# The first scaling of raw weight words in the attention stage, made by GpSimd

## The chip, the cores and the metric

The kernel runs on one core of one Trainium2 chip. A core has TensorE (PE, matmuls; PEld is its weight load), VectorE (DVE), ScalarE (ACT), GpSimd (POOL) and SyncE (SP, which issues DMAs). The metric is the device time of one execution in microseconds; the kernel before takes 1007.44 us (median of 3 runs, 1006.85 to 1007.59).

## The reference, cut to what matters

Attention with a cumulative bias, then two feed-forward layers, the first with a product of two projections, the second with a squared ReLU:

```python
scores = scale * q @ k.T                      # 4 batches, 8 heads, S = 576, D = 64
scores = where(causal, -1e9, scores + minimum(cum_j - cum_i, 0))   # cum: cumsum(relu(s))
x = softmax(scores) @ v                       # -> 2304 tokens x 512
x = ((x @ w_a) * (x @ w_b)) @ w_out           # 512 -> 1536 -> 512
r = maximum(x @ w_in2, 0)                     # 512 -> 2048
out = (r * r) @ w_out2                        # -> 512
```

The weights come in as double precision numbers, that is as pairs of 32-bit words, and are made on the chip into a high and a low part of single precision.

## The kernel before, in words

**Arithmetic.** Every large matmul is made of three: high by high, high by low, low by high. So each operand is held twice. The low parts come from a subtraction of the rounded high part.

**Decoding a weight block.** A block of 128 x 512 weights is decoded by `words` (L1002) and `decode` (L1031), in this chain: SP loads 512 KB of raw words; the high words, read as floats, are scaled by 2^-112 in place (the "first scaling", L1015: by DVE or ACT, whichever the planner finds free sooner); DVE shifts and masks the high words into a new tile, then merges the sign; the low words are scaled by 2^-29 (ACT or DVE); POOL or DVE adds them in; ACT casts the sum to the high part `wh`; POOL or DVE subtracts for the low part (`wl`, `wlo`). The first layer has 36 such blocks, `split_w(f)` for f = 0 to 11, each with its three matrices; the raw words lie in tiles named `words`, `roomxh` and `roomxl`. The loads of the first six blocks (f below 2) are `held`. The second layer's blocks go through `quarters` (L1061), which calls `words` too: those of w_in2 in a stream called "late" (tiles `w2ir`), those of w_out2 later (tiles `w2or`).

**Stages by time.** 0 to 50 us: attention of the first batch. 50 to about 395: the first feed-forward layer on the first chunks of tokens, whose weight blocks are decoded as they are needed, woven with the attention of the second to fourth batch and with the "late" decoding of the second layer's w_in2. To 640: the rest of the first layer. 640 to 1010: the second layer, whose `first` (L1526) loads two prepared blocks of w_in2 (`w_3_0`, `w_3_1` from scratch `w2q`) and makes the products `pa`, `pb`, `pc`, and whose `second` multiplies by w_out2 (tiles `ws_*` from `w2s`) into `po_*`. `quads` (L1306) loads the second layer's inputs (`yr`) and splits them.

**Names.** In the instruction orders below the leading digit of a name (batch, chunk) is left out and a running number follows: `ab_9_0` is the w_a product of weight block f = 9, `g_8` the gated result of block 8, `py` the first layer's output product, `st` and `se` scores, `pt` and `tt` transposed exponentials, `av` and `ae` weighted values, `tav` the same for the first batch's last rows, `rs` the transpose of the row sums, `yd` the first layer's output on its way to the second.

**What sets the order.** Nothing of the order is written by hand. `Plan` (L73) records every operation with the engines that may make it and a cost for each, and `order` (L148) simulates the engines with those costs and sorts all operations by their planned start; L267 then issues them. The costs for n elements a row are 150 + each x n ns on DVE, 190 + 0.833 n on ACT, 110 + 2.3 n on POOL, and 3 ns for each KB of a load. A cost is thus no time, but it decides which engine makes an operation and when each is issued. Where the plan lets PE idle for over `GAP` (400 ns) before the first product into a fresh bank, `order` notes idle/`BURN` (230 ns) matmuls on a constant tile, and L262 issues them there ("warm" matmuls):

```python
gap = t - max(free[e], min(op.bank.tag.free))
if gap > self.GAP:
    op.idle = max(op.idle, int(gap / self.BURN))
...
for _ in range(op.idle if warm else 0):
    w = warm.get()
    eng.matmul(op.bank.get(), w[:, : w.shape[0]], w, start=True, stop=True)
```

Of the kernel before, what the change touches and what calls it, by code (L numbers as in the profile page):

```python
# [7 lines left out]
F32 = mybir.dt.float32  # L8
# [5 lines left out]
ALU = mybir.AluOpType  # L14
# [255 lines left out]
def attention_moe_moe(tc, q, k, v, s, w_a, w_b, w_out, w_in2, w_out2, out):  # L270
# [18 lines left out]
    CW = 384  # L289
# [18 lines left out]
    pl = Plan(nc)  # L308
# [27 lines left out]
    def scratch(shape, dtype, name):  # L336
        return pl.fixed(lambda: pools["dram"].tile(shape, dtype, name=name))
# [17 lines left out]
    def on_dve(method, n, *args, two=False, each=1.04, **kw):  # L355
        return "DVE", 150 + each * n, two, method, args, kw

    def on_act(method, n, *args, psum=False, **kw):
        return "ACT", (155 if psum else 190) + 0.833 * n, False, method, args, kw

    def on_gps(method, n, *args, **kw):
        return "POOL", 110 + 2.3 * n, True, method, args, kw

    def dve(*args, reads=(), **kw):
        pl.call(on_dve(*args, **kw), reads=reads)
# [7 lines left out]
    def dma(out, in_, kb, takes=(), lag=0.0):  # L373
        pl.call(("SP", max(kb * 3.0, 170.0), False, "dma_start", (out, in_), {}), takes=takes, lag=lag)
# [5 lines left out]
    def copy(n, out, in_, psum=False, by="AD"):  # L380
        ways = []
        if "A" in by:
            ways.append(on_act("copy", n, out, in_, psum=psum))
        if "D" in by:
            ways.append(on_dve("tensor_copy", n, out, in_, two=not psum, each=1.04 if psum else 0.52))
        pl.call(*ways)

    def subtract(n, out, a, b, by="PD"):
        kw = {"out": out, "in0": a, "in1": b, "op": ALU.subtract}
        ways = []  # L390
        if "P" in by:
            ways.append(on_gps("tensor_tensor", n, **kw))
        if "D" in by:
            ways.append(on_dve("tensor_tensor", n, two=True, **kw))
        pl.call(*ways)
# [590 lines left out]
    def quad(nm):  # L986
        return gated("lop", [P, 2 * CW], F32R, "yq", 14, nm)
# [14 lines left out]
    def words(w, by_col, f, raw, t, takes=(), held=False):  # L1002

        f0 = 2 * f * P
        n = ND * P
        if by_col:
            src = w[:, f0 : f0 + 2 * P].rearrange("(d p) c -> p d c", p=P)
        else:
            src = w[f * P : f * P + P, :].rearrange("p (d c) -> p d c", d=ND)
        dma(raw.rearrange("p (d c) -> p d c", d=ND), src, 540 if pl.stream == "late" else 680, takes, HOLD if held else 0.0)  # L1010
        pairs = raw.rearrange("p (n w) -> p n w", w=2)
        low, high = pairs[:, :, 0], pairs[:, :, 1]

        hf = high.bitcast(F32)
        pl.call(  # L1015
            on_dve("tensor_scalar", n, hf, hf, 2.0**-112, None, op0=ALU.mult, two=True, each=0.52),
            on_act("mul", n, hf, hf, 2.0**-112),
        )
        dve(
            "tensor_scalar", n, t, high, 3, 0x7FFFFFF8, op0=ALU.logical_shift_left, op1=ALU.bitwise_and, two=True,  # L1020
            each=0.52,
        )
        dve("scalar_tensor_tensor", n, t, high, -0x80000000, t, op0=ALU.bitwise_and, op1=ALU.bitwise_or, two=True)
        pl.call(
            on_act("activation", n, low, low.bitcast(U32), AF.Copy, scale=2.0**-29),
            on_dve("tensor_scalar", n, low, low.bitcast(U32), 2.0**-29, None, op0=ALU.mult, two=True, each=0.52),
        )
        kw = {"out": t, "in0": t, "in1": low, "op": ALU.add}
        pl.call(on_gps("tensor_tensor", n, **kw), on_dve("tensor_tensor", n, two=True, **kw))
# [12 lines left out]
    w2q = [[scratch([P, 7 * QW], F32, f"w2q{j}_{z}") for z in range(2)] for j in range(PAIRS)]  # L1042

    def temp(dtype, nm):
        return gated("lop", [P, 2 * DM], dtype, "tmp", 4, nm)
# [260 lines left out]
    def quads(nm, source):  # L1306

        n = 2 * CW

        def pull(k, h):  # L1310
            x = temp(F32, f"yr{nm}_{k}{h}")[:, :n]
            for d in range(2):
                for at_, m, src in source(2 * k + d, h):
                    dma(x[:, d * CW + at_ : d * CW + at_ + m], src, m * 0.5)
            return x

        b11, b21, b22, b12 = (pull(k, h) for k, h in ((0, 0), (1, 0), (1, 1), (0, 1)))
        lo, hi = {}, {}

        def split(x, v):  # L1320
            lo[x], hi[x] = quad(f"{x}l{nm}"), quad(f"{x}h{nm}")
            copy(n, hi[x], v)
            subtract(n, lo[x], v, hi[x].bitcast(F32))

        split("b11", b11)
        split("b21", b21)
        split("b22", b22)
        combine(n, b22, b22, b12)
        combine(n, b12, b12, b11)
        combine(n, b11, b11, b22, ALU.add)  # L1330
        combine(n, b21, b21, b11)
        for x, v in (("t2", b11), ("t1", b12), ("t3", b22), ("t4", b21)):
            split(x, v)
        return {x: [t[x].rearrange("p (d c) -> p d c", d=2) for t in (hi, lo)] for x in hi}
# [191 lines left out]
    def first(t0, j, left, held):  # L1526

        nm = f"{t0}_{j}"
        pair = j % 2
        yq = y_quads[t0]  # L1530
        w = [block(f"w{nm}_{z}") for z in range(2)]
        for z in range(2):
            dma(w[z].rearrange("p q c -> p (q c)").bitcast(F32), w2q[j][z], 896)

        def times(ps, q, start=True):
            i = SEVEN.index(q)
            product(ps, [[x[:, i, d * P : d * P + P] for d in range(2)] for x in w], yq[q], start)

        def bank_(k):
            if t0 == 0 and j == 1:  # L1540
                return gated("po", [P, 512], F32, "po", 5, f"p{k}{nm}")[:, :CW]
            return mm_bank(f"p{k}{nm}")[:, :CW]

        v1, v3 = (x[:, :CW] for x in halves(f"v{nm}a", F32))
        v2, v4 = (x[:, :CW] for x in halves(f"v{nm}b", F32))

        def squared(v, ps, s):
            if s is None:
                urgent(act, "activation", CW, v, ps, AF.Relu, psum=True)
            else:  # L1550
                urgent(dve, "tensor_tensor", CW, out=v, in0=ps, in1=s, op=ALU.add)
                pl.call(
                    on_act("activation", CW, v, v, AF.Relu),
                    on_dve("tensor_scalar_max", CW, v, v, 0.0, two=True, each=0.52),
                )
            kw = {"out": v, "in0": v, "in1": v, "op": ALU.mult}
            pl.call(on_act("activation", CW, v, v, AF.Square), on_dve("tensor_tensor", CW, two=True, **kw))
            return v

        def split(q, v):  # L1560
            if q in ROOM:
                if pair == 0:
                    held[q] = flat(ROOM[q], 1, f"g{nm}{q}")
                hi, lo = (held[q][:, 2 * pair + z, :CW].part((pair, z)) for z in range(2))
            else:
                hi, lo = (flat("wh", 3 * NF1, f"g{nm}{q}{z}")[:, :CW] for z in range(2))
            left[q, pair] = hi, lo
            copy(CW, hi, v, by="A")
            subtract(CW, lo, v, hi.bitcast(F32))

        def keep(tag, bufs, width, k, ps):
            t = sb([P, width], F32, tag, bufs, f"{k}{nm}")[:, :CW]
            urgent(act, "copy", CW, t, ps, psum=True)
            return t

        a = bank_("a")
        times(a, "b11")
        s1 = keep("a", 2, 512, 1, a)
        b = bank_("b")
        times(b, "b21")  # L1580
        b11 = squared(v1, b, s1)
        times(a, "t2", False)
        s2 = keep("lo1", 1, DM, 2, a)
        b = bank_("c")
        times(b, "t1")
        times(a, "t3", False)
        s3 = keep("a", 2, 512, 3, a)
        b22 = squared(v3, b, s3)
        times(a, "t4", False)
        b21 = squared(v2, a, None)  # L1590
        times(b, "b22", False)
        b12 = squared(v4, b, s2)
        split("b11", b11)
        split("b22", b22)
        split("b21", b21)
        combine(CW, b22, b22, b12)
        combine(CW, b12, b12, b11)
        combine(CW, b11, b11, b22, ALU.add)
        combine(CW, b21, b21, b11)
        for q, v in (("t3", b22), ("t1", b12), ("t2", b11), ("t4", b21)):  # L1600
            split(q, v)
# [113 lines left out]
    for t0 in range(0, NT, 2 * CW):  # L1715
        for j in range(PAIRS):
            if j % 2 == 0:
                left, held = {}, {}
# [56 lines left out]
```

## Time and profile before

| | |
|---|---|
| median of 3 runs | 1007.44 us (1006.85 to 1007.59) |
| the profiled execution | 1012.5 us, its span 1010.7 us, mean TensorE clock 0.996 |
| busy in the span | PE 98%, PEld 85%, DVE 73%, ACT 58%, POOL 35% |
| DMA | 242.94 MB, mean 240 GB/s |

The profiled execution is 5.1 us longer than the median of the runs, and 1.8 us of it lie outside the span. Terms worked out from the trace are added to the profiled execution, and the sum is carried to the median. PE is busy almost all the time, so what counts is the few stretches in which it idles or has a lower clock, and whatever is put on PE or taken from it.

### The profile page before, as it was taken

Reading aid. Unit: us, or ns where it says so; the run is one execution under the profiler, and the core shown is the slowest. Engines: PE = TensorE matmul, PEld = TensorE weight load, DVE = VectorE, ACT = ScalarE, POOL = GpSimd, SP = SyncE. Lnnn points to the kernel's source line nnn. Section 1 sums busy time; section 2 is a strip of 40 time slices with the busy share of each in tenths; the row PEclk is TensorE's granted clock in tenths of the full one; section 3 lists DMA queues with packets and bytes.
Section 4 is the critical chain, followed back from the end, with each engine's and each line's share of the span. In section 5 each row is a group of like instructions: output and inputs, shape, how many; then the busy total and the mean of one; then the engine's idle time right before and its main releaser. Section 6 shows DMA issues by size and latency. Waiting matters only on the chain.

```text
span 1010.7 us, 16505 instructions
## 1 busy us (share of the span) xinstructions
PE 990.0 (98%) x5565; PEld 854.8 (85%) x5568; DVE 733.0 (73%) x1499; ACT 584.1 (58%) x1289; POOL 350.4 (35%) x317
## 2 busy tenths in 40 slices
PE   9999999999999999999999999999989999999998
PEld 5567777777777787888889999999989999999998
DVE  5887787867678677386888886657877755876566
ACT  6776776656565564242444443666656766657552
POOL 2543444443344533020233332314544221531122
PEclk9999999999999999999999999999999999999999
DMA  7677787587788778767577557587979976688664
GB/s 218 188 224 243 237 264 237 167 260 240 225 236 252 209 218 265 234 180 264 170 255 229 184 174 275 177 303 253 359 276 328 314 271 229 235 286 301 230 238 167
DMA packets 136972, 242.94 MB, mean 240 GB/s; under 512 B 16204, under 2 KB 87992, under 8 KB 136888
## 3 DMA queue, kind: packets, MB, share of 16 engines
q1 hardware_dynamic: 133688, 235.99, 70.8%
q10 hardware_dynamic: 3200, 5.90, 2.3%
q8 instruction: 44, 0.72, 0.3%
q14 instruction: 40, 0.33, 0.1%
HBM read 183.78 MB, written 52.11 MB: 233 GB/s over the span
## 4 chain that ended last, share of the span: by engine, by line
PE 89%; DMA 5%; DVE 3%; ACT 1%; issue 1%; SPq 1%; POOL 0%; ACTq 0%; DVEq 0%; POOLq 0%
PE ab L267 18%; PE py L267 10%; PE pa L267 9%; PE po_0t L267 6%; PE st L267 5%; PE pc L267 5%; PE wa L267 5%; PE pw L267 4%; PE pt L267 3%; PE av L267 3%; PE wc L267 2%; PE pb L267 2%; PE po_0b L267 2%; PE po_1b L267 2%; PE po_3b L267 2%; PE po_2b L267 1%
## 5 line engine op out<-in xcount | busy, mean ns | idle before, releaser
L267 PE MATMUL py<-g,wh 128*128 128x512 f32 x288 | 92.2, 401 | 0.0
L267 PE MATMUL ab<-xh,wh 128*128 128x512 f32 x192 | 77.6, 404 | 0.0
L267 PE MATMUL ab<-xh,lo 128*128 128x512 f32 x192 | 75.1, 391 | 0.0
L267 PE MATMUL ab<-xl,wh 128*128 128x512 f32 x192 | 74.8, 390 | 0.0
L267 PE MATMUL ab<-x,wh 128*128 128x512 f32 x192 | 64.1, 414 | 0.6 <-POOL x L267 0.6
L267 PEld LDWEIGHTS py<-g,wh 128*128 128x128 f32 x288 | 53.5, 191 | 11.2 <-issue 0.7
L267 DVE CUSTOM_DVE_ANT_0 st<-st,mask 128x512 f32<-128x512 f32 (+2 forms) x96 | 46.7, 502 | 21.3 <-PE st L267 16.2
L267 PE MATMUL py<-g,loo 128*128 128x512 f32 x144 | 56.7, 394 | 0.0
L267 PE MATMUL st<-fk,fq 65*128 65x384 f32 (+3 forms) x128 | 42.5, 443 | 0.9 <-ACT a L267 0.7
L267 ACT COPY a<-ab 128x512 f32<-128x512 f32 x36 | 21.2, 588 | 38.0 <-PE ab L267 37.9
L267 POOL TENSOR_TENSOR w2ip<-w2it,w2ip 128x512 fp32r<-128x512 f32 (+1 forms) x20 | 22.8, 1147 | 58.5 <-ACT w2ip L267 38.4
L267 PEld LDWEIGHTS ab<-xh,lo 128*128 128x128 f32 x192 | 36.0, 188 | 7.8
L267 PE MATMUL av<-ph,val 128*64 128x512 f32 (+3 forms) x256 | 41.5, 445 | 0.0
L267 DVE COPY ph<-pt 128x512 f32<-128x512 f32 (+1 forms) x53 | 31.1, 588 | 14.1 <-PE pt L267 11.9
L267 PEld LDWEIGHTS ab<-xl,wh 128*128 128x128 f32 x192 | 36.2, 189 | 5.9
L267 PEld LDWEIGHTS ab<-xh,wh 128*128 128x128 f32 x192 | 36.2, 188 | 5.9
L267 ACT COPY ph<-pt 128x512 f32<-128x512 f32 (+1 forms) x43 | 22.3, 527 | 31.6 <-PE pt L267 23.5
L267 PEld LDWEIGHTS ab<-x,wh 128*128 128x128 f32 x192 | 33.4, 189 | 7.7 <-issue 1.8
L267 PEld LDWEIGHTS av<-ph,val 128*64 128x64 f32 x256 | 15.5, 136 | 26.4 <-issue 23.7
L267 PE MATMUL ab<-x,wl 128*128 128x512 f32 x96 | 37.8, 394 | 0.0
L267 DVE TENSOR_TENSOR ab<-ab,a 128x512 f32<-128x512 f32 x36 | 25.1, 697 | 16.8 <-PE ab L267 13.9
L267 POOL TENSOR_TENSOR wl<-roomxl,wh 128x512 fp32r<-128x512 f32 x19 | 25.8, 1359 | 30.3 <-ACT wh L267 23.1
(743 smaller groups left out, 3300.0 us busy)
## 6 DMA issues: line engine op xcount, KB each, us to landing
w<-w2q SPq DMA_DIRECT2D x48, 896.0 KB
lo<-wlab SPq DMA_DIRECT2D x36, 512.0 KB
w2q<-w2ip SPq DMA_DIRECT2D x48, 256.0 KB
w2s<-w2op SPq DMA_DIRECT2D x48, 256.0 KB
loo<-wlo SPq DMA_DIRECT2D x24, 384.0 KB
w2ir<-in_moe_w_in SPq DMA_DIRECT2D x16, 512.0 KB
w2or<-in_moe_w_out SPq DMA_DIRECT2D x16, 512.0 KB
ws_0t<-w2s SPq DMA_DIRECT2D x12, 512.0 KB
```

The source lines that it names most:

```text
L267: getattr(eng, method)(*map(real, args), **{k: real(a) for k, a in kw.items()})
```

## The change

Three edits. The first scaling in `words` is given to POOL alone, unless the stream is "late" or the load is held: 34 scalings (30 blocks f = 2 to 11, and four of w_out2). In `quads` the planner's cost of the input loads goes from 0.5 to 0.3 of their width, and in `first` that of the w_in2 loads from 896 to 760; both change no transfer, only the planner's idea of it.

```diff
--- before.py
+++ after.py
@@ -1013,8 +1013,10 @@
 
         hf = high.bitcast(F32)
         pl.call(
+            *((on_gps("tensor_scalar", n, hf, hf, 2.0**-112, None, op0=ALU.mult),) if pl.stream != "late" and not held else (
             on_dve("tensor_scalar", n, hf, hf, 2.0**-112, None, op0=ALU.mult, two=True, each=0.52),
             on_act("mul", n, hf, hf, 2.0**-112),
+            )),
         )
         dve(
             "tensor_scalar", n, t, high, 3, 0x7FFFFFF8, op0=ALU.logical_shift_left, op1=ALU.bitwise_and, two=True,
@@ -1311,7 +1313,7 @@
             x = temp(F32, f"yr{nm}_{k}{h}")[:, :n]
             for d in range(2):
                 for at_, m, src in source(2 * k + d, h):
-                    dma(x[:, d * CW + at_ : d * CW + at_ + m], src, m * 0.5)
+                    dma(x[:, d * CW + at_ : d * CW + at_ + m], src, m * 0.3)
             return x
 
         b11, b21, b22, b12 = (pull(k, h) for k, h in ((0, 0), (1, 0), (1, 1), (0, 1)))
@@ -1530,7 +1532,7 @@
         yq = y_quads[t0]
         w = [block(f"w{nm}_{z}") for z in range(2)]
         for z in range(2):
-            dma(w[z].rearrange("p q c -> p (q c)").bitcast(F32), w2q[j][z], 896)
+            dma(w[z].rearrange("p q c -> p (q c)").bitcast(F32), w2q[j][z], 760)
 
         def times(ps, q, start=True):
             i = SEVEN.index(q)
```

The first place is on PE in the attention of the second batch, about 166 us, where the products of weight block 9 begin. Before:

```order
L267 MATMUL ae_2_2008<-tph_2_0_1992,val_2_1599 64x64 x8
L267 MATMUL ae_2_2008<-tph_2_1_1996,val_2_1599 64x64 x2
L267 MATMUL rs_2_2021<-ident,one_2_1800 9x128
L267 MATMUL ab_8_1_1998<-x_549,wh_1_1789 128x512 x2
L267 MATMUL ab_8_1_1998<-x_549,wl_1754 128x512
L267 MATMUL ab_9_0_2034<-x_406,wh_0_1924 128x512 x2
L267 MATMUL ab_9_0_2034<-x_406,wl_1943 128x512
L267 MATMUL ab_8_1_1998<-x_696,wh_1_1789 128x512 x2
```

After, with the first two of sixteen warm pairs shown and the rest left out:

```order
L267 MATMUL ab_8_1_1959<-x_859,wh_1_1877 128x512 x2
L267 MATMUL ab_8_1_1959<-x_859,wl_1859 128x512
L267 MATMUL ae_2_2001<-tph_2_0_1990,val_2_1598 64x64 x8
L267 MATMUL ae_2_2001<-tph_2_1_1992,val_2_1598 64x64 x2
L267 MATMUL rs_2_2016<-ident,one_2_1805 9x128
L262 LDWEIGHTS warm
L262 MATMUL ab_9_0_2046<-warm 128x512
...
L267 MATMUL ab_9_0_2046<-x_406,wh_0_2036 128x512 x2
L267 MATMUL ab_9_0_2046<-x_406,wl_2041 128x512
```

The products of block 8 now stand ahead of the transpose `rs_2`, and sixteen warm matmuls between it and block 9. ACT's order around the cast of block 9's high part (`wh_0`), before:

```order
L267 COPY ph_2_1_0_1910<-pt_2_1_0_1889 128x512
L267 COPY a_7_1918<-ab_7_0_1771 128x512
L267 CAST wh_0_1924<-roomxl 128x512
L267 ACTIVATE te_2_1937,sum_209<-se_2_0_1878,neg_204 128x288
L267 ACTIVATE te_2_1937,sum_209<-se_2_1_1884,neg_204 128x288
L267 CAST wh_1_1956<-roomxl 128x512
```

And after:

```order
L267 COPY u_2_2019<-av_2_1939 128x512
L267 COPY rows_2_2024<-rs_2_2016 9x128
L267 CAST g_8_2026<-ab_8_1_1959 128x512
L267 CAST wh_0_2036<-roomxl 128x512
L267 CAST wh_1_2039<-roomxl 128x512
```

The cast stood ahead of the exponentials `te` of the second batch; now it stands behind the copy of the transposed row sums and the cast of `g_8`. The second place is on PE where the third batch's attention begins, about 210 us. Before:

```order
L267 MATMUL st_0_1_1_2502<-t2k_0_1_2403,t2q_0_1_2398 128x128
L267 MATMUL pt_0_0_0_2514<-ident,a_0_0_2481 128x128 x2
L267 MATMUL pt_0_0_0_2514<-ident,b_0_0_2462 128x128
L267 MATMUL pt_0_0_0_2514<-ident,c_0_0_2444 128x128
L267 MATMUL ab_11_1_2483<-x_549,wh_1_2288 128x512 x2
L267 MATMUL ab_11_1_2483<-x_549,wl_2253 128x512
L267 MATMUL ab_11_1_2483<-x_696,wh_1_2288 128x512 x2
L267 MATMUL ab_11_1_2483<-x_696,wl_2253 128x512
L267 MATMUL st_0_1_2_2536<-T_2286 128x256
...
L267 MATMUL ab_11_1_2483<-x_868,wh_1_2288 128x512 x2
L267 MATMUL ab_11_1_2483<-x_868,wl_2253 128x512
L267 MATMUL se_0_0_2555<-T_2286 128x288
```

And after:

```order
L267 MATMUL st_0_1_1_2531<-t2k_0_1_2448,t2q_0_1_2403 128x128
L267 MATMUL pt_0_0_0_2540<-ident,a_0_0_2505 128x128 x2
L267 MATMUL pt_0_0_0_2540<-ident,b_0_0_2498 128x128
L267 MATMUL pt_0_0_0_2540<-ident,c_0_0_2465 128x128
L267 MATMUL st_0_1_2_2551<-T_2409 128x256
L267 MATMUL st_0_1_2_2551<-t2k_0_1_2448,t2q_0_1_2403 128x256
L267 MATMUL se_0_0_2579<-T_2409 128x288
```

The three groups of block 11's products between the scores have moved ahead of them. The third place is SP's queue where the second layer begins, about 660 us. Before:

```order
L267 DMA yd_7140<-yo_4_7281 128x256 x2
L267 DMA w_3_0_7317<-w2q_0_3937 128x1792
L267 DMA w_3_1_7323<-w2q_1_3972 128x1792
L267 DMA ws_0b_7349<-w2s_5519 128x1024
L267 DMA ws_0b_7363<-w2s_5519 128x1024
L267 DMA yd_7140<-yo_5_7325 128x256 x2
L267 DMA w_4_0_7431<-w2q_0_4460 128x1792
L267 DMA w_4_1_7433<-w2q_1_4496 128x1792
```

And after:

```order
L267 DMA yd_7168<-yo_4_7305 128x256 x2
L267 DMA ws_0b_7331<-w2s_5550 128x1024
L267 DMA yd_7168<-yo_5_7340 128x256 x2
L267 DMA w_3_0_7368<-w2q_0_4016 128x1792
L267 DMA ws_0b_7373<-w2s_5550 128x1024
L267 DMA w_3_1_7384<-w2q_1_4030 128x1792
L267 DMA ws_0b_7409<-w2s_5550 128x1024
L267 DMA ws_0t_7429<-w2s_5550 128x1024
L267 DMA w_4_0_7477<-w2q_0_4482 128x1792
```

A block of `ws` and the last write of `yd` now go ahead of `w_3`, and the two halves of `w_3` have a `ws` between them.

## Rows read from the trace of the kernel before

**Rows 1.** The page, part 1: busy us, share of span, instructions.
```profile
PE 990.0 (98%) x5565; PEld 854.8 (85%) x5568; DVE 733.0 (73%) x1499; ACT 584.1 (58%) x1289; POOL 350.4 (35%) x317
```

**Rows 2.** By stage: length, busy PE, PEld, DVE, ACT, POOL, PE clock, DMA, GB/s.
```profile
50.00:200.00 150.00, 149.44 (x861) 107.15 (x859) 117.80 (x294) 107.63 (x254) 65.18 (x52) 1.00 0.73 226
200.00:225.00 25.00, 23.16 (x142) 17.68 (x139) 16.17 (x44) 14.23 (x37) 11.85 (x9) 0.93 0.87 261
...
640.00:760.00 120.00, 114.40 (x641) 111.42 (x640) 84.83 (x150) 78.17 (x164) 45.06 (x37) 0.99 0.82 292
760.00:1010.00 250.00, 245.23 (x1414) 244.59 (x1412) 173.32 (x302) 149.32 (x310) 72.17 (x66) 1.00 0.73 260
```

**Rows 3.** Groups of ACT, 50 to 200 us: count, busy us, mean ns, idle before.
```profile
L267 ACT ACTIVATE roomxh<-roomxh 128x512 f32<-128x512 f32 x10 | 6.8, 682 | 2.4 <-DMA roomxh<-in_moe_w_out 2.1 <-DMA roomxh<-in_moe_w_b 0.3
...
L267 ACT CAST g<-ab 128x512 fp32r<-128x512 f32 x11 | 6.4, 584 | 4.3 <-DVE ab L267 4.3
```

**Rows 4.** Groups of DVE, 50 to 200 us.
```profile
L267 DVE TENSOR_TENSOR ab<-ab,a 128x512 f32<-128x512 f32 x11 | 7.7, 695 | 4.1 <-ACT wh L267 2.3 <-PE ab L267 1.8
...
L267 DVE TENSOR_TENSOR wl<-wt,wh 128x512 fp32r<-128x512 f32 x2 | 1.4, 686 | 0.1
...
L267 DVE TENSOR_SCALAR words<-words 128x512 f32<-128x512 f32 x1 | 0.4, 425 | 0.0
```

**Rows 5.** Groups of POOL, 50 to 200 us.
```profile
L267 POOL TENSOR_TENSOR roomxl<-roomxl,roomxh 128x512 int32<-128x512 int32 x7 | 9.1, 1299 | 11.4 <-ACT roomxh L267 8.4 <-DMA wlo<-wl 3.0
```

**Rows 6.** Groups of POOL, 0 to 20 us.
```profile
L267 POOL MEMSET maskf<- 128x512 f32 x1 | 0.5, 531 | 0.0
```

**Rows 7.** The chain of waits, 8 to 12 us: start, us, what.
```profile
8.71 1.29 PE st L262 x6
```

**Rows 8.** PE's timeline near 166 us: start, us, engine, line, operation.
```profile
166.01 0.28 PE L267 MATMUL rs<-ident,one 128*9 128x128 f32 x1
...
166.83 0.39 PE L267 MATMUL ab<-x,wh 128*128 128x512 f32 x1
```

**Rows 9.** ACT's timeline, near 158 and 205 us.
```profile
157.71 0.63 ACT L267 CAST wh<-roomxl 128x512 fp32r<-128x512 f32 x1
...
205.14 0.26 ACT L267 COPY rows<-rs 9x128 f32<-9x128 f32 x1
```

**Rows 10.** PE's timeline, 209 to 214 us; in brackets idle before and its releaser.
```profile
209.42 0.63 PE L267 MATMUL ab<-x,wh 128*128 128x512 f32 x2
...
210.12 0.28 PE L267 MATMUL st<-T 66*128 66x256 f32 x1
...
212.22 0.40 PE L267 MATMUL se<-T 66*128 66x288 f32 x1 [0.99 <-ACT a L267]
...
213.87 0.40 PE L267 MATMUL se<-T 66*128 66x288 f32 x1 [0.85 <-ACT a L267]
```

**Rows 11.** Two stretches, columns as in rows 2.
```profile
214.00:220.00 6.00, 6.00 (x29) 5.26 (x30) 3.69 (x11) 3.99 (x9) 5.03 (x4) 0.72 0.65 186
745.00:755.00 10.00, 8.82 (x42) 8.82 (x43) 5.97 (x8) 5.25 (x11) 3.18 (x2) 0.83 0.40 140
```

**Rows 12.** PE's waits, 640 to 760 us: total, times, longest.
```profile
PE pc L267 <- DVE v_7a L267: 1.9, 1, 1.9
PE po_2t L267 <- DMA ws_2t<-w2s: 1.4, 1, 1.4
PE pa L267 <- ACT 20_2_7365 L267: 0.9, 1, 0.9
```

**Rows 13.** SP's queue, near 661 us.
```profile
660.83 0.88 SPq L267 DMA_DIRECT2D w<-w2q x2
```

**Rows 14.** DVE's timeline, 743 to 749 us.
```profile
743.12 2.55 DVE L267 TENSOR_TENSOR b11l<-yr,b11h 128x768 fp32r<-128x768 f32 x1
...
748.38 0.96 DVE L267 TENSOR_TENSOR b22l<-yr,b22h 128x768 fp32r<-128x768 f32 x1 [2.25 <-ACT b22h L267]
```

**Rows 15.** POOL's timeline, 743 us.
```profile
743.02 1.83 POOL L267 TENSOR_TENSOR b21l<-yr,b21h 128x768 fp32r<-128x768 f32 x1 [0.89 <-ACT b21h L267]
```

## The prediction

> **What bounds the kernel now.** I read the page's busy shares first: TensorE (PE) is busy 990.0 us, 98% of the span [rows 1], VectorE (DVE), ScalarE (ACT) and GpSimd (POOL) 73%, 58% and 35%. So time can go or come in two ways only: PE gets more or fewer instructions, or it idles or loses clock for longer or shorter. Then the busy time by stage [rows 2]: of the attention stage's 150 us from 50 to 200, PE works 149.44; from 200 to 225 it idles 1.84 at a mean clock of 0.93; from 640 to 760 it idles 5.60; from 760 to the end 4.77. What the change makes lighter or heavier on ACT, DVE and POOL is on no path by itself. From 50 to 200 nothing is to be gained, and a wait made there is paid.
>
> **The engines' own work.** The two instruction orders count 34 scalings on POOL (30 of the first layer's 36 weight blocks, and 4 blocks of the second layer's w_out), 24 of which ACT made before and 10 DVE. In turn the planner takes 21 two-input operations off POOL and 5 copies off ACT, all to DVE. The counts close: POOL +34-21 = +13, ACT -24-5 = -29, DVE -10+21+5 = +16. One ACT scaling is 0.682 us [rows 3], one on DVE 0.425 [rows 4]; ACT gets 24 x 0.682 = 16.4 us lighter before its copies. No row shows a scaling on POOL. From above it is bounded by POOL's two-input operation on the same tile, 1.299 us [rows 5], from below by a fill of a 128x512 tile, which reads nothing, 0.531 [rows 6]. I take 1.3, the nearer row, since a scaling reads as well as writes. POOL then changes by 34 x 1.3 - 21 x 1.3 = +17 us (at 0.53 by -9), in a stage where it is busy 65.18 of 150 us [rows 2]. Both ends cost nothing, because PE's work covers them: a block's first product comes some 8 us after its cast (below). Were that cover gone, each block would cost what a POOL scaling is longer than the old one, 0.6 us, and 30 blocks 18 us; the range doesn't hold that, since PE's new order was laid with POOL at 1.29 us an operation. What costs something is what this lengthened chain did to the order.
>
> **Term 1, inserted warm matmuls.** Where the planner expects PE to idle for more than 400 ns, it writes matmuls on a warm tile into the program, one for each 230 ns. They run whether the gap is there or not. Six of them take 1.29 us [rows 7], 0.215 each. The order has 72 instead of 44. 16 new ones stand ahead of the first product of weight block 9 (ab_9_0). Before, PE goes there from the row-sum transpose at 166.01 through products of block 8 to block 9 at 166.83 with no gap [rows 8]: its weight was cast at 157.71 [rows 9], some 8 us earlier. Now block 8's products are all ahead of that transpose, and ACT makes the copy after the transpose (0.26 by its row), the cast of g_8 (0.584 by its group) and only then the block's cast (0.63), some 1.5 us, with DVE's low part 0.69 behind it [rows 3, 4, 9]. So 16 x 0.215 = 3.44 us of PE outlast the true wait of 1.5 to 2.2 us, and the whole of 3.4 is paid, as there was none before. At py_3_0_0, near 345 us, ten stand instead of five. There the last product of block 11 must pass DVE's multiply (0.695), ACT's cast (0.584) and DVE's subtract (0.69), 2.0 us, and ten fill 2.15: the five more cost 1.1. Two ahead of tav_2 cost 0.4. Of the rest (3 ahead of tav_0 and 2 ahead of av_2_0) I think that they fill waits that stand there anyway: 0. Term 1 is 3.4 + 1.1 + 0.4 = +4.9, and with 0.2 for hand-overs +5.1. It is bounded by 28 x 0.215 = 6.0 above and, if all were waits otherwise, by the new waits alone, some 1.5 + 1 = 2.5 below.
>
> **Term 2, the start of the third batch (212 us).** Before, PE waits here twice for a softmax exponential of ACT, 0.99 and 0.85 us [rows 10], and behind that has a mean clock of 0.72 for 6 us [rows 11], between its two levels of 1.2 and 2.4 GHz: 0.28 x 6 = 1.7 us lost. Together 3.5. In the order before, three groups of products of block 11 stand between the last scores and the se scores; now they stand ahead of them, and scores follow on scores. Such a group of three matmuls takes 0.70 us (210.12 less 209.42 in [rows 10]), so PE comes 2.1 us earlier to the same softmax and waits that much longer: +2.0. The bounds: -2.0, if ACT, relieved of its scalings, has the exponentials earlier and the clock stays up (1.7 and a little of the idle), and +4.0, if the longer idle also costs 2 us more at the lower clock.
>
> **Term 3, 640 to 760 us.** Only the two planner costs of the loads act here. PE idles 5.60 us and loses 0.17 x 10 = 1.7 of clock after 745 [rows 2, 11], so 7.3 is all there is to get. The waits: 1.9 for DVE's v_7a, 1.4 for a load of ws, 0.9 for ACT's cast, and smaller ones [rows 12]. SP's queue issued w_3 at 660.83 ahead of ws_0b [rows 13]; now a ws_0b goes before w_3, later blocks of w are issued earlier among the ws loads, and PE's order alternates the first and second products differently. I let all waits but v_7a's go, 5.6 - 1.9 = 3.7, less 0.2 left over: 3.5. The v_7a wait has another cause: DVE's b11l took 2.55 us, where its like b22l took 0.96 [rows 14], and it ended after POOL's b21l, which ran from 743.02 to 744.85 [rows 15]. Whether the two meet again depends on a microsecond or so, so I count half of the wait, 0.9, and half of the clock, 0.85. Against this stands a new succession of dependent products at the sixth block, which I price like the 0.9 wait for a cast. Term 3 is -3.5 - 0.9 - 0.8 + 0.9 = -4.3, with -7.3 and -1.0 as ends.
>
> **Elsewhere.** From 400 to 638 us PE's order is unchanged word for word, and from 760 on nearly so: 0, with 0.5 either way.
>
> **The sum** is 5.1 + 2.0 - 4.3 = +2.8 us. Against the profiled execution's 1012.5 (span 1010.7 and 1.8 around it) that is 1015.3. That execution is 5.1 above the median of the runs, 1007.44, so the forecast for the median is 1010.2 us.
>
> **Rivals.**
> 1. PE keeps its clock at both places and the loads' order pays in full: term 3 -7.3, term 2 only its clock, -1.7. With +5.1 it is -3.9, 1003.5: faster. It decides from where terms 2 and 3 bring over 7.1 together. For it: the waits of 640 to 760 are for single transfers and one collision. Against: scores behind scores in term 2.
> 2. The terms cancel: term 2 at 0, as ACT's relief makes good what the fillers gave; +0.8, 1008.2.
> 3. POOL holds DVE up. The collision of [rows 14, 15] shows that a DVE operation with two inputs waits out a POOL operation. Of 13 more POOL operations each may hold a DVE one for half of 1.3 us, 8.5 us of DVE; DVE has 41 us idle from 50 to 225 [rows 2], so a quarter at most should reach PE, 2.1 on top of the forecast: +4.9, 1012.3. It decides where the operation held up is the subtract or the mask that PE waits for. The Trainium skill, "SBUF — State Buffer", section "Who interferes with whom", says that the two engines share a port pair as an exclusive lock, that a DVE instruction with two inputs in SBUF, or in a two-port mode, contends with POOL's reads, and that whichever issues second fully blocks. By that rule scalings moved to POOL cost DVE more than their own time; the 2.55 against 0.96 us agrees.
> 4. The change does nothing in time: warm matmuls and scalings all lie in waits, 1007.4. Against: 149.44 of 150 us busy.
>
> **How the numbers follow.** About 0.2%, 2 us, is what a measurement of this kernel can tell from no change. Forecast 0.40 (0.36 slower, 0.04 within), rival 1 0.29 (faster), rival 2 0.17 (same), rival 3 0.09 (slower), rival 4 0.05 (same). So faster 0.29, same 0.26, slower 0.45. The forecast's own range is 1007.5 to 1013; the wider one reaches to rival 1's time below (1003.2) and past rival 3's above (1014.5, the forecast with term 2 at +4 and term 3 at -2).
>
> **What would show it.** Term 1: sixteen warm matmuls of about 3.4 us ahead of the first product of block 9, and PE busy about 5 us longer in all. Term 2: waits of PE for ACT near 215 us of over 3 us in sum, and a clock below 0.93 there. Term 3: from 640 to 760 us PE idle near 2 us in place of 5.6, and no wait for ws or w over 0.5. Rival 3: DVE operations of the attention stage longer than before at their mean. Wrong would be: PE's busy time unchanged up to 400 us, or a wait of PE for POOL's scaled words between 50 and 225.

## The result, and the profile after

The changed kernel takes 1018.6 us (median of 4 runs, 1017.56 to 1020.2) beside 1007.52 of the kernel before. The medians are 11.1 us apart; the ratio over the runs is 1.0103, 95% interval [1.0082, 1.0123], +10.4 us. Timed again beside 23 runs of before it came to 1018.52 and 1.0089 [1.0058, 1.0119], +9.0. Slower was forecast, 1010.2 us or +2.8; it is slower by 9 to 11. Its profiled execution took 1018.01 us (span 1016.2), and the forecast's sum for that was 1015.3.

The page of the changed kernel, part 1, and its stages (columns as in [rows 2]); they answer to [rows 1, 2]:

```profile
PE 995.3 (98%) x5589; PEld 856.6 (84%) x5596; DVE 744.0 (73%) x1515; ACT 569.5 (56%) x1260; POOL 376.9 (37%) x330
```

```profile
50.00:200.00 150.00, 149.84 (x862) 106.06 (x863) 119.41 (x290) 95.07 (x232) 81.97 (x58) 1.00 0.71 219
200.00:225.00 25.00, 22.00 (x125) 16.71 (x124) 19.15 (x49) 14.29 (x38) 12.54 (x10) 0.86 0.74 206
640.00:760.00 120.00, 118.29 (x683) 116.53 (x682) 89.02 (x154) 80.56 (x166) 49.69 (x39) 1.00 0.81 291
760.00:1010.00 250.00, 246.94 (x1418) 245.28 (x1417) 174.35 (x304) 147.80 (x308) 73.35 (x67) 1.00 0.72 256
```

PE is busy 5.3 us longer and the span 5.5. From 200 to 225 it idles 3.00 in place of 1.84 at a lower clock; from 640 to 760 it idles 1.71 in place of 5.60.

The first place, block 9, on PE and ACT of the changed kernel (start, us, operation; [rows 8, 9] before):

```profile
168.77 0.28 PE L267 MATMUL rs<-ident,one 128*9 128x128 f32 x1
169.10 3.40 PE L262 MATMUL ab<-warm 128*128 128x512 bf16 x15
172.15 0.82 PE L267 MATMUL ab<-x,wh 128*128 128x512 f32 x2
```

```profile
169.09 0.25 ACT L267 COPY rows<-rs 9x128 f32<-9x128 f32 x1 [0.34 <-PE rs L267]
169.25 0.57 ACT L267 CAST g<-ab 128x512 fp32r<-128x512 f32 x1
169.75 1.14 ACT L267 CAST wh<-roomxl 128x512 fp32r<-128x512 f32 x2
```

The warm matmuls run 3.4 us (one of the sixteen records is missing); ACT's copy, cast of g and casts of block 9 are done at 170.9. Without the warm matmuls 1.37 us of wait stand here (e4 below); the rest of the 3.4 is burnt.

The second place, the start of the third batch, on PE of the changed kernel ([rows 10, 11] before):

```profile
216.06 0.28 PE L267 MATMUL st<-t2k,t2q 128*128 128x256 f32 x1
218.50 0.61 PE L267 MATMUL se<-T 66*128 66x288 f32 x1 [2.17 <-ACT a L267]
```

```profile
215.00:220.00 5.00, 2.83 (x16) 2.34 (x15) 3.46 (x13) 3.88 (x11) 0.41 (x1) 0.77 1.06 244
220.00:225.00 5.00, 4.68 (x21) 3.53 (x22) 3.85 (x13) 3.37 (x8) 2.87 (x3) 0.55 0.64 178
```

Scores on scores, as feared: a wait of 2.17 us for ACT's exponential, and then the granted clock falls to a mean of 0.77 and 0.55 between its levels of 1.2 and 2.4 GHz, 5 x 0.23 + 5 x 0.45 = 3.4 us lost where before it was 1.7.

### The profile page after: what moved, and what is told of

It is laid out like the page before. It is cut to its first block, busy times and chain, and to the rows that moved or that the text cites. A ratio compares the mean times of both kernels' runs of the same rounds, so it can differ in the third digit from the quotient of the medians.

```text
span 1016.2 us, 16556 instructions
## 1 busy us (share of the span) xinstructions
PE 995.3 (98%) x5589; PEld 856.6 (84%) x5596; DVE 744.0 (73%) x1515; ACT 569.5 (56%) x1260; POOL 376.9 (37%) x330
## 4 chain that ended last, share of the span: by engine, by line
PE 86%; DMA 6%; DVE 4%; ACT 2%; issue 1%; POOL 1%; SPq 0%; ACTq 0%; DVEq 0%; POOLq 0%
PE ab L267 17%; PE py L267 9%; PE pa L267 9%; PE po_0t L267 6%; PE st L267 5%; PE pc L267 5%; PE wa L267 5%; PE pw L267 4%; PE pt L267 3%; PE av L267 3%; DMA w<-w2q 3%; PE wc L267 2%; PE pb L267 2%; PE po_0b L267 2%; PE po_2b L267 2%; PE po_1b L267 2%
## 5 line engine op out<-in xcount | busy, mean ns | idle before, releaser
L267 ACT COPY ph<-pt 128x512 f32<-128x512 f32 (+1 forms) x51 | 26.3, 523 | 34.7 <-PE pt L267 32.5
L267 POOL TENSOR_TENSOR w2it<-w2it 128x256 f32<-128x256 f32 x16 | 11.7, 733 | 67.7 <-DMA w2q<-w2ip 47.0
L267 DVE COPY ph<-pt 128x512 f32<-128x512 f32 (+1 forms) x45 | 26.3, 586 | 13.2 <-PE pt L267 11.6
L267 DVE TENSOR_TENSOR y<-py,y 128x512 f32<-128x512 f32 x36 | 24.6, 687 | 13.1 <-PE py L267 12.8
```

The costliest lines, as they stand in the source:

```text
L267: getattr(eng, method)(*map(real, args), **{k: real(a) for k, a in kw.items()})
```

## The experiments

Each kernel was timed beside the kernel before on the same chip: e1 to e4 on one chip, e5 to e8 on a second, e9 to e12 on a third. Before itself spreads from 1005.3 to 1015.2 us over those runs (medians of 1009.0 to 1009.4, each of 22 or 23 runs), so a single profiled execution can stand some 5 us to either side of the median. All ratios are to the kernel before on the same chip, and the last column is the ratio put into microseconds.

| kernel | ratio, 95% interval | us |
|---|---|---|
| before, a copy | 1.0002 [0.9986, 1.0018] | 0 |
| changed | 1.0089 [1.0058, 1.0119] | +9.0 |
| GpSimd edit alone | 1.0068 [1.0045, 1.0092] | +6.9 |
| both load costs alone | 0.9984 [0.9963, 1.0004] | -1.6 |
| changed, without the 28 new warm matmuls | 1.0064 [1.0043, 1.0086] | +6.5 |
| before's order, scalings on GpSimd | 1.0015 [0.9995, 1.0036] | +1.5 |
| changed order, scalings on ACT | 1.0113 [1.0082, 1.0143] | +11.4 |
| w load cost alone | 1.0017 [0.9995, 1.0040] | +1.7 |
| input load cost alone | 0.9952 [0.9934, 0.9970] | -4.8 |
| GpSimd edit and input load cost | 1.0056 [1.0036, 1.0076] | +5.7 |

**e1, before again.** No edit.

> The kernel before, unchanged, profiled a second time. Its runs take 1007.5 us, its first profiled execution took 1012.5, and the changed kernel's profiled execution (1018.0) is like its runs (1018.6). Theory A: the first profile of before caught 5 us that its ordinary runs don't have, and these are the losses of 640 to 760 us (5.6 us idle, 1.7 us of clock) that my third term counted as to be gained. Then this profile comes at about 1007.5, its PE idle from 640 to 760 is near 1.5 us, and the stretches up to 400 us are as in the first profile within 0.5 us. Rival B: profiling itself costs this kernel 5 us everywhere or in another stage: a profile of 1012 again, with 5 us of idle from 640 to 760 again.

Neither came out clean: 1009.05 in the median of 12, but this profiled execution was a long one again (1011.7, the longest of the 12), with 4.5 us of idle from 640 to 760 and the wait for v_7a again. Nothing about short executions could be read from it.

**e2, the GpSimd edit alone**, the first hunk of the diff.

> Only the first edit (scaling by GpSimd), both planner costs as before. Theory A (the cost lies before 400 us: warm matmuls, the start of the third batch; the loads' costs gain nothing against ordinary runs): 1016 to 1019 us, +9 to +11. Rival B (the planner costs of the loads make the ordinary runs slower by some 5 us): 1012 to 1014.

1015.62, +6.9 [4.5, 9.3], a little below A's band and above B's. Most of the cost is this edit's. The loads' costs seem to add some 2 on top (the intervals overlap), which theory A had left at nothing.

**e3, both load costs alone**, the other two hunks.

> Only the two planner costs of the loads, scaling as before. PE's order before 475 us is that of the kernel before. Theory A: within 1.5 us of before, 1006 to 1009. Rival B: 1011 to 1013. My third term as predicted: 1003.

1008.51, -1.6: inside theory A's band, just outside its 1.5. My third term's 1003 is out, rival B too.

**e4, without the new warm matmuls.**

```diff
-                    op.idle = max(op.idle, int(gap / self.BURN))
+                    op.idle = max(op.idle, int(gap / self.BURN) if t < 50e3 else 0 if t < 330e3 else min(int(gap / self.BURN), 5))
```

> The changed kernel without the 28 warm matmuls that its plan has more than before (sixteen ahead of block 9, three, two and two elsewhere, five of the ten at 350 us), the order of all else unchanged. If the warm matmuls are paid as my first term has it: 4 to 5 us less than the changed kernel, about 1014. If the waits that they fill are as long: 0 to 1 less. If the idle PE loses clock in place of them: 1 less to 3 more.

1015.25, +6.5 in place of +9.0, between the first two expectations: 2.5 of the 28 x 0.215 = 6.0 us come back (the two intervals overlap). PE at block 9 then, and its waits from 200 to 235:

```profile
168.46 0.28 PE L267 MATMUL rs<-ident,one 128*9 128x128 f32 x1
170.11 0.73 PE L267 MATMUL ab<-x,wh 128*128 128x512 f32 x2 [1.37 <-ACT wh L267]
```

```profile
PE se L267 <- ACT a L267: 2.2, 1, 2.2
PE st L267 <- ACT c L267: 0.9, 2, 0.5
PE py L267 <- DMA loo<-wlo: 0.4, 1, 0.4
```

Where 3.4 us were burnt stands a wait of 1.37 us. So the new order has a real wait here, and the warm matmuls cost 2 us more than it. Where three stood ahead of `tav_0` and two ahead of `av_2_0`, PE goes on in e4 without a wait (at 66.57 and 221.47 us).

**e6, before's order with GpSimd at work, and e7, the changed order with ACT.** The plan is made as before (as after), and only when the instructions are issued does another engine get the scaling:

```diff
-            for method, args, kw in op.ways[op.eng][1]:
+            for method, args, kw in op.ways[op.eng][1] if op.to is None else [op.to[3:]]:
...
+        if pl.stream != "late" and not held:
+            op.to = on_gps("tensor_scalar", n, hf, hf, 2.0**-112, None, op0=ALU.mult)
```

In e7 the last line is `op.to = on_act("mul", n, hf, hf, 2.0**-112)`.

> The kernel before with its order of instructions kept, but the same 34 scalings issued to GpSimd at the places that the old plan gave them (31 of them are taken from ACT, 3 from DVE). Theory A (the cost is the order that the new planner costs make): within 2 us of before. Rival B (the cost is GpSimd itself: a scaling takes 1.67 us in the changed kernel's trace, against 0.68 on ACT, and holds DVE up at the shared port): 5 us or more above before.

> The changed kernel with its order kept, but its 34 scalings issued to ACT at the places where the plan has them on GpSimd. Theory A (order): within 2 us of the changed kernel. Rival B (GpSimd itself): 5 us or more below it, near before.

+1.5 us [-0.5, 3.6], not clear of before, and +11.4, not clear of the changed kernel. This settles the main question: the engine that scales costs 3.6 us at most and perhaps nothing, ACT in its place gives nothing back, and the order that the planner makes from its cost is nearly all of it. The place where PE begins the first layer's last output products (`py`, behind the fillers near 394 us) says the same. It lies at 391.2 to 394.5 us in the six traces with before's order up to there and before's engines (before, e1, e3, e8, e9, e11), and at 400.4 to 405.7 in the six with the changed order and its fillers (changed, e2, e5, e7, e10, e12). e4 has 398.3, and e6 397.3, in an execution 2.6 us longer than its median. GpSimd's largest group of scalings from 50 to 400 us, first of the changed kernel, then of e6:

```profile
L267 POOL TENSOR_SCALAR words<-words 128x512 f32<-128x512 f32 x11 | 18.5, 1686 | 16.8 <-DMA words<-in_moe_w_out 4.7 <-DVE wt L267 4.4 <-DMA words<-in_moe_w_a 3.8
```

```profile
L267 POOL TENSOR_SCALAR words<-words 128x512 f32<-128x512 f32 x12 | 21.4, 1780 | 4.3 <-DMA words<-in_moe_w_a 2.1 <-DMA tk<-in_k 1.6 <-DMA words<-in_moe_w_b 0.6
```

A scaling takes 1.7 to 1.8 us there, against 0.68 on ACT, and neither trace has a wait of PE for one.

**e5, the changed kernel again**, for a trace and for times on the same chips.

> The changed kernel, unchanged, profiled a second time and timed beside the kernel before on the same chip (before took 1005.4 to 1014.5 us there, median 1009.4). If the cost is the 6 to 8 us that stand in the traces at 394 us (first layer's last output product: 394.3 and 394.5 before, 400.4 with the GpSimd edit alone, 402.2 in the changed kernel), with what the loads' order gains from 640 to 760 given back behind 760: 1016 to 1018. If the 11 us of the first comparison are all the change's: 1020.

1018.52, between the two expectations; the profiled execution was the shortest of six, 1015.97.

**e8, the w load cost alone; e9, the input load cost alone; e10, GpSimd edit and input load cost.** One or two hunks of the diff each.

> Only the planner's cost of the w_in2 loads, 760 in place of 896. The two costs together came to 1008.5, 1.6 us below before without being clear of it. In their trace PE gains 3 us from 638 to the second chunk's start near 750 and gives 2 back there after in waits for w. If this cost makes both: 1007 to 1009. If it makes the waits for w alone: 1010 to 1012, with waits of PE for w of 0.8 or more near 780 and 900 us.

> Only the planner's cost of the second layer's input loads (0.3 in place of 0.5), scaling and w loads as before. In the traces every kernel with the w cost of 760 idles PE 2.6 to 5.3 us behind 760 us, mostly in waits for w, those without it 0.9 to 2.2. Theory A: the give-back is the w cost's, so this kernel has under 2.2 us of idle there and, if it keeps the shorter stretch of 640 to 760 us, takes 1005 to 1008. Rival: the give-back comes with any earlier start of the second chunk: idle of 3 us or more behind 760, 1008 to 1010.

> The GpSimd edit with the input loads' cost, without the w cost. The GpSimd edit alone came 6.9 us above before, the whole change 9.0. Theory A (the w cost takes 2 us back): 1015 to 1016.5, PE idle behind 760 us below 2.2. If the difference of 6.9 and 9.0 is scatter: 1017 to 1019.

1010.61 (the w cost's waits alone), 1004.94 and 1015.57 (theory A in both), with e9 just below its band and its idle behind 760 us 2.3 where under 2.2 was expected. The w cost adds 3.2 us to the input load cost (-4.8 to -1.6) and 3.3 to it with the GpSimd edit (+5.7 to +9.0); the intervals overlap, barely in the first pair, and alone it is not clear of before. The edits do not add up: +6.9, -4.8 and +1.7 make +3.8, and the whole change has +9.0. The input load cost gains 4.8 alone and 1.2 with the GpSimd edit (+6.9 to +5.7). PE's waits behind 765 us with the w cost alone (first) and with the input load cost alone:

```profile
PE pa L267 <- DMA w<-w2q: 3.0, 2, 1.6
PE pc L267 <- DVE v_0a L267: 0.9, 1, 0.9
```

```profile
PE pc L267 <- DVE v_0a L267: 0.9, 1, 0.9
```

The orders show the reason. Before, the products of block 3 of w_in2 (`pa_3`) in the second and third chunk stand amid the products `po_0b11`; with the cheaper w cost they stand ahead of these, right behind `pa_2`, as the plan thinks that their load lands sooner. The edit changes nothing in the load itself. In e8 the two halves of w are issued at 775.09, and PE stands for 1.40 us until 784.13:

```profile
775.09 1.25 SPq L267 DMA_DIRECT2D w<-w2q  x2
```

```profile
784.13 0.61 PE L267 MATMUL pa<-b11h,w 128*128 128x384 f32 x2 [1.40 <-DMA w<-w2q]
```

The input load cost alone is faster than both kernels, by 0.48% [0.30, 0.66] against before.

**e11 and e12, one more trace of either kernel.**

> The kernel before, one more profiled execution. Its runs reach from 1005.4 to 1015.2 us, and both traces so far are of long ones (1012.5, 1011.7). If the spread is in the stretch of 640 to 760 us, a short execution (under 1008.5) shows below 3.5 us of PE idle there; if it is in the clock losses of 1.7 us and in waits for loads all over, the stretch stays at 4.5 to 5.6.

> The changed kernel, one more profiled execution (traces so far of 1018.0 and 1016.0). By the traces: first layer's last output product (before 394 us) at 401 to 403, so +7 to +8, PE idle of 1.4 to 1.8 us from 640 to 760, and 3 to 4 behind 760.

e11 is the short execution that was wanted, 1007.66 us, and is like the runs that the prediction was compared with (1006.85 to 1007.59); e12 took 1019.87. By stage, e11 first (columns as in [rows 2]):

```profile
0.00:50.00 50.00, 46.96 (x244) 26.70 (x247) 34.77 (x82) 35.45 (x92) 21.06 (x41) 1.00 0.77 205
50.00:200.00 150.00, 149.34 (x857) 106.73 (x855) 118.95 (x294) 106.86 (x252) 65.37 (x53) 1.00 0.72 226
200.00:235.00 35.00, 33.35 (x219) 25.78 (x218) 23.61 (x68) 21.04 (x54) 16.74 (x12) 1.00 0.92 284
235.00:400.00 165.00, 164.17 (x1006) 129.97 (x1006) 120.09 (x317) 95.64 (x249) 67.44 (x56) 1.00 0.76 230
400.00:640.00 240.00, 236.67 (x1203) 210.14 (x1202) 178.08 (x295) 98.85 (x172) 64.12 (x58) 1.00 0.64 212
640.00:760.00 120.00, 116.23 (x664) 113.50 (x663) 85.09 (x155) 79.28 (x167) 46.89 (x38) 1.00 0.86 307
760.00:1000.00 240.00, 239.03 (x1377) 238.18 (x1376) 166.18 (x290) 146.52 (x305) 69.02 (x63) 1.00 0.73 258
```

```profile
0.00:50.00 50.00, 46.61 (x244) 26.34 (x247) 35.09 (x80) 36.53 (x94) 24.67 (x44) 1.00 0.74 205
50.00:200.00 150.00, 149.84 (x860) 106.06 (x861) 119.00 (x290) 94.70 (x232) 82.19 (x59) 1.00 0.71 219
200.00:235.00 35.00, 30.86 (x191) 22.37 (x192) 27.18 (x63) 17.23 (x44) 16.77 (x12) 0.95 0.76 217
235.00:400.00 165.00, 163.55 (x1007) 130.36 (x1006) 118.37 (x324) 95.58 (x250) 72.64 (x60) 1.00 0.77 238
400.00:640.00 240.00, 236.94 (x1191) 208.23 (x1191) 179.72 (x300) 97.79 (x171) 56.91 (x52) 1.00 0.67 220
640.00:760.00 120.00, 118.37 (x683) 116.64 (x682) 89.22 (x154) 80.73 (x166) 49.31 (x39) 1.00 0.81 294
760.00:1000.00 240.00, 234.74 (x1348) 233.14 (x1347) 163.21 (x286) 146.55 (x306) 68.93 (x63) 1.00 0.72 261
```

These two tables close the account of one pair of executions, a little wider apart than the medians: the spans are 1005.9 and 1018.1, 12.2 us. PE's additional warm matmuls are 28 x 0.215 = 6.0. Idle time is a length less PE's busy time: from 200 to 235 it grows from 1.65 to 4.14, +2.5, and the clock there costs 0.05 x 35 = 1.75 where e11 lost none; from 640 to 760 it shrinks from 3.77 to 1.63, -2.1; behind 760 it grows from 0.97 to 5.26, +4.3; the other four stretches come to +0.2. Sum: 6.0 + 2.5 + 1.75 - 2.1 + 4.3 + 0.2 = 12.6. By the pages PE is busy 994.2 in place of 987.0 and so idles 5.0 longer, which agrees with the idle terms. The two terms at 760 belong together, since e12 is some 10 us late there and one wait of 0.7 (for v_0a, at 762.55) has slipped behind the mark: +2.2 in sum. PE's waits behind 760 us in e12:

```profile
PE pa L267 <- DMA w<-w2q: 3.2, 2, 2.0
PE pc L267 <- DVE v_0a L267: 1.5, 2, 0.9
PE po_0t L267 <- DMA ws_3t<-w2s: 0.6, 1, 0.6
```

For e11 the expectation had two answers and got neither whole: 3.8 us of idle from 640 to 760, between them, and no clock lost anywhere. For e12 the first layer was about as expected (403.1 for the product that stands at 394.3 in the first trace of before; at 392.6 in e11), the idle behind 760 was more than expected.

## Why the prediction was wrong in size

**The bound and the main rule were right.** PE is the bound; ACT's busy time fell by 14.6 us (584.1 to 569.5) and that gave nothing; the order paid. Rivals 1, 2 and 4 are out. Rival 3's 1012.3 lies nearest to the measured time, but its cause costs little (below). The measured time lies beyond the wider range's end, 1014.5, too. (That range gives rival 1's time as 1003.2; its own sum makes it 1003.5.)

**Term 1 (+5.1): right in mechanism, 6.0 in PE's time.** The five that I had let fall into waits were paid too, by e4. As worked out, the new order has a wait of its own under the sixteen (1.37 us, forecast 1.5 to 2.2), so taking all 28 out brought back only about 2.5, with overlapping intervals. The fillers at `py_3_0_0` start at 393.6 us in before's first trace and at 400.4 in the changed kernel's, not near 345.

**Term 2 (+2.0): right in mechanism, too small.** In e11 and e12 it is +4.2, in the two first profiled executions 6.4 (3.0 and 3.4) against 3.5, +2.9. The idle is near what was worked out (1.85 + 2.1): 3.0 in the first trace, 4.1 in e12, where a wait of 1.1 for DVE (`tt`) is part of it. What was mis-sized is the clock: it falls here in all three traces of the changed kernel, in the first for twice as long, and in two of the three of before.

**The step from the profiled execution to the median failed, and term 3 (-4.3) with it.** The step was "That execution is 5.1 above the median of the runs, 1007.44, so the forecast for the median is 1010.2 us". The sum for the profiled execution, 1015.3, is 2.7 below what was measured; the forecast for the median is 8.4 below. Against the trace that it was read from, term 3 came out larger than forecast: the idle from 640 to 760 fell by 3.9 and the 1.7 of clock is not lost there, -5.6 in all, though a wait of 0.99 for w stayed. But part of what it gained is what made that execution long. The v_7a wait of 1.9, the 1.7 of clock behind it and the 1.7 of clock at 215 us make 5.3, and e11, an execution of 1007.66, has none of the three. So some of these microseconds were counted as a gain of the change, and then all 5.1 were taken off once more, when the runs I forecast against don't have these losses. Against e11 term 3 is -2.1. The changed kernel has no such surplus: its profiled executions took 1018.0, 1016.0 and 1019.9, around its medians of 1018.5 and 1018.6. The three runs behind the 1007.44 were short ones besides: on the other chips before's median is 1009.0 to 1009.4.

Part of what makes an execution long is one collision. The wait for v_7a is in the three long traces of the old second-layer order (1012.5, 1011.7, 1013.3), at 1.9, 1.9 and 2.2 us; it is not in e11, nor in any of the ten traces of other second-layer orders. In e11 DVE's b11l started 0.24 us ahead of POOL's b21l and ran its 0.96; in [rows 14, 15] POOL's began 0.10 ahead, and DVE took 2.55. DVE and POOL in e11:

```profile
740.97 0.96 DVE L267 TENSOR_TENSOR b11l<-yr,b11h 128x768 fp32r<-128x768 f32 x1
```

```profile
741.21 2.41 POOL L267 TENSOR_TENSOR b21l<-yr,b21h 128x768 fp32r<-128x768 f32 x1 [1.24 <-ACT b21h L267]
```

The Trainium skill, "SBUF — State Buffer", section "Who interferes with whom", has the sentence "Issue order, not op shape, decides who blocks". Both traces agree: 2.55 against 0.96 us for the same DVE operation, 1.83 against 2.41 for POOL's. In e1 and e6 POOL's began 0.2 ahead as well, and DVE took 2.4. This one event doesn't carry the whole spread of before's executions. e1's span is 4.0 us longer than e11's, but its idle from 640 to 760 only 0.7; the rest is 1.7 of clock near 215 us and a wait of 1.3 for a ws load behind 760.

**"... and from 760 on nearly so: 0" failed.** The differences that I passed over were the products of block 3 put ahead of their load: about 3.2 us by e3 and e9, and in e12 3.2 of the 4.3 are waits for w. "Only the two planner costs of the loads act here" failed too. The GpSimd edit alone lays another order in the second layer, and its trace idles 1.9 us from 640 to 760; so the loads' gain there was not to be had a second time (1.2 us with it, 4.8 without).

**All terms together, by the three traces of either kernel.** The second layer's first product `pa` starts at 638.3, 638.3 and 636.4 us before and at 647.3, 645.0 and 646.6 after, 8.6 later at the mean, where terms 1 and 2 had 7.1. From there to the end of the span it takes 372.5, 371.6 and 369.5 us before and 369.0, 369.2 and 371.5 after, 1.3 less at the mean, where term 3 had 4.3.

**A count was wrong, at no cost.** Set beside e6, which keeps before's order, the 34 scalings were 31 of ACT's and 3 of DVE's, not 24 and 10; the totals by engine stand. GpSimd's busy time grew by 26.5 us (350.4 to 376.9), not by 17, since a scaling takes longer than the 1.3 us taken for it.

**Rival 3, POOL holding DVE up, happens and hardly reaches PE.** DVE's shift `roomxl<-roomxh` (512 columns) from 50 to 225 us in before, e6 and the changed kernel:

```profile
L267 DVE TENSOR_SCALAR roomxl<-roomxh 128x512 int32<-128x512 int32 x8 | 4.1, 516 | 0.0
```

```profile
L267 DVE TENSOR_SCALAR roomxl<-roomxh 128x512 int32<-128x512 int32 x8 | 4.9, 610 | 0.0
```

```profile
L267 DVE TENSOR_SCALAR roomxl<-roomxh 128x512 int32<-128x512 int32 x8 | 5.6, 706 | 0.0
```

PE idles 1.81 us from 50 to 200 in e6, where before has 0.56 and one wait (for `x`, 0.6). PE's waits there in e6:

```profile
PE ab L267 <- POOL x L267: 0.5, 1, 0.5
PE tt L267 <- DVE ph L267: 0.5, 1, 0.5
PE se L267 <- ACT a L267: 0.4, 1, 0.4
PE tav L267 <- DVE tph L267: 0.2, 1, 0.2
```

So some 1.2 us of it may reach PE there. From 235 to 400 PE waits 3.1 us in e6 for ACT's `c` (0.5 in before); the longest of these waits, 2.0 at 312 us, goes back to a load of `raw_1k` for which DVE stood 2.5 us, and not to a scaling. What may be POOL's is within e6's +1.5, and far from the cost of the change.

## What to carry to other kernels

Where a planner lays the order, an edit that changes a cost or an engine is an edit of the order: diff the orders to the end, and price every product that moves ahead of its load or away from its filler. To know whether engine or order is at fault, keep the plan and switch the engine when the instructions are issued, and the other way round. A profiled execution that is longer than the runs holds losses which the runs don't have: find them and take them out before counting any as to be gained, and don't carry a sum to the median by the difference of the two alone.

## What was not expected of the hardware

A scaling of every second word of a 1024-word row took GpSimd 1.57 to 1.78 us by group means in the changed kernel's first trace and in e6, more than its two-input operation on the same tiles (1.30), which I had taken as the upper bound. And the clock's losses near 213 to 221 us came as 1.7 us or twice that, during or just behind waits of PE for ACT of 0.9 to 2.2 us, but not behind each such wait: e11 idled 1.65 us from 200 to 235 at a clock of 1.00.
